# Query tiles copied inside SBUF by a transfer and transposed as float32r

## The chip, the cores and the metric

One core of a Trainium2 chip runs the whole kernel. The metric is the device time of one execution in microseconds. Engines: TensorE (PE; its weight loads are PEld), VectorE (DVE), ScalarE (ACT), GpSimd (POOL), and SyncE (SP), which issues the transfers.

## The reference

x is 2048 x 512 in float32. It is normalised, goes through a linear attention with 32 heads of 16 and, beside it, through a gated feed-forward block of width 1792; the two results are multiplied.

```python
xn = _layernorm(x)
q, k, v = split_heads(xn @ wqkv)            # 32 heads of 16
pq, pk = phi(q), phi(k)                     # phi(t) = (t + 1 if t > 0 else exp(t)) + 1e-6
kv = einsum("hsd,hse->hde", pk, v)
den = einsum("hqd,hd->hq", pq, pk.sum(axis=s)) + 1e-6
s = (einsum("hqd,hde->hqe", pq, kv) / den) @ wo
g = silu((gelu(xn @ w_gate) * (xn @ w_up)) @ w_down)
out = x + s * g
```

## The kernel before

Large products run on TensorE in float32r, with each float32 operand split into a high and a low part (three products for one), and blocks of 2 x 2 are multiplied with seven products instead of eight. A float32r matmul here has 128 x 128 weights and 512 moving columns.

The program has four stretches: normalisation, keys, queries and the state (up to about 135 us); the feed-forward block for one half of the tokens (p = 1, to about 330 us) and the small matrices of the attention; the feed-forward block for the other half (p = 0, 352 to 545 us); and the last stage S, which multiplies the scaled queries with a combined matrix and writes the output.

No engine's order is written out. The kernel records operations with `do(engine, cost, function, output, inputs)`, each with an estimated cost in us, and the class Plan searches an order for all engines at once from costs, dependences and estimated transfer times (a list schedule, improved in rounds with a fixed seed). Each engine then executes its list in that order; SP issues the transfers in its own list's order and waits there for what a transfer needs.

The sixteen query tiles (128 tokens x 512) are dealt with in pairs by `queries(i)`, spread over the p = 0 block. For a pair with first token tile t0: the queries are loaded from device memory (q_d) into the buffer q (place 12 of the pool "dp"); POOL multiplies each tile with the keys' sum into u (place 13); DVE adds over each head (den), adds den_eps, takes the reciprocal (rr) and scales q in place (L1142); TensorE transposes each tile in four 128 x 128 pieces into a PSUM bank ptq (L1148), as float32 against the identity matrix; ACT copies it into pT (place 14); and a transfer stores pT in device memory (pn_d), from where stage S loads it much later (tiles pb). Places 12, 13 and 14 are single buffers: the next pair uses the same ones. For half p = 1 tokens 1024 to 2047 come first, so the first pair is q8 with tiles 8 and 9.

Names in rows: FX, FY, FZ are PSUM banks of the feed-forward's first products, DX, DY, DZ those of its second, w and wd their weights, hf the split hidden values, acc the sums in SBUF. Numbers behind a name (FX11, ptq10) count units or token tiles.

Of the kernel before, what the change touches and what calls it, by code (L numbers as in the profile page):

```python
# [11 lines left out]
F32 = mybir.dt.float32  # L12
F32R = mybir.dt.float32r
AF = mybir.ActivationFunctionType
ALU = mybir.AluOpType
AX = mybir.AxisListType

P = 128
EPS_LN = 1e-5
EPS = 1e-6  # L20
WARM = 11
WARM2 = 2
ENGINES = {mybir.EngineType.PE, mybir.EngineType.Activation, mybir.EngineType.DVE, mybir.EngineType.Pool}


# [339 lines left out]
def kernel(  # L365
# [13 lines left out]
    nc = tc.nc  # L379
    S, D = x.shape  # L380
# [3 lines left out]
    KT = D // P  # L384
# [29 lines left out]
    def ring(tag, places):  # L414
        n = count[tag] = count.get(tag, -1) + 1
        return places[n % len(places)]
# [12 lines left out]
    def bank(i, name, shape=(P, D)):  # L429
        return tile_in("ps", i, list(shape), F32, name)  # L430


    def D2(i, name, dtype=F32, shape=(P, 2, D), parts=2):
        return tile_in("dp", i, list(shape), dtype, name, parts)
# [13 lines left out]
    def dma(dst, src, kb, name=""):  # L448
        do("SP", 0.475, lambda o, i: nc.sync.dma_start(o, i), dst, src, kb=kb, name=name)
# [22 lines left out]
    def copy(eng, dst, src, n, name=""):  # L472
        if eng == "ACT":
            do("ACT", act(n), lambda o, i: nc.scalar.copy(o, i), dst, src, name=name)  # L474
        else:
            do("DVE", dve(n), lambda o, i: nc.vector.tensor_copy(o, i), dst, src, name=name)
# [36 lines left out]
    do("POOL", 0.6, lambda o: nc.gpsimd.memset(o, NT * EPS), zacc)  # L513
    den_eps = tile_in("sm", "de", [P, H], F32, "den_eps")

    def warm(o, w, n=WARM):
        for _ in range(n):
            nc.tensor.matmul(o, w, w, start=True, stop=True)
# [54 lines left out]
    def half(v, i):  # L573
        return v.part(v.res[i:i + 1], (slice(None), i))
# [53 lines left out]
    xns = {}  # L628
# [31 lines left out]
    def transp(n, i):  # L660
        t = tokens[n][i]
        pt = early.get((n, i)) or bank(1, f"pt{t}", (P, KT, P))

        def run(o, a, b):
            for k in range(KT):
                nc.tensor.transpose(o[:, k, :], a[:, k * P:(k + 1) * P], b)  # L666
        do("PE", 0.432, run, pt, xns[t], ident, key=("T", n, i), name="T")
        if i == 0:
            xts[n] = D2(3 + n % 3, f"xt{n}").map(lambda ap: ap.rearrange("p a (k c) -> p a k c", c=P))
        v = xts[n]  # L670
        xts[n, i] = v.part((v.res[i],), (slice(None), i))
        copy("ACT", xts[n, i], pt, D, f"xt{n}{i}")
        pts[n, i] = pt
# [447 lines left out]
    def heads(v):  # L1121
        return v.map(lambda ap: ap.rearrange(heads_ap, d=DH))

    def queries(i):

        t0 = [8, 10, 12, 14, 0, 2, 4, 6][i]
        q, w, pT = D2(12, f"q{t0}"), D2(13, f"u{t0}"), D2(14, f"pT{t0}")
        for n in range(2):
            t = t0 + n
            dma(half(q, n), q_d(t, slice(t * P, (t + 1) * P)), 256)  # L1130
        den = little("den", f"den{t0}", [P, 2, H])
        for n in range(2):
            tt("POOL", "mul", heads(half(w, n)), heads(half(q, n)), heads(zb), D, "u")
        for n in range(2):
            do("DVE", 0.602, lambda o, i: nc.vector.tensor_reduce(o, i, axis=AX.X, op=ALU.add), den[:, n], heads(half(w, n)), name="den").port = False
        do("DVE", 0.1, lambda o, i: nc.vector.tensor_add(o, o, i.unsqueeze(1).to_broadcast([P, 2, H])), den, den_eps, name="eps").port = True
        r = little("rr", f"rr{t0}", [P, 2, H])
        do("DVE", 0.275, lambda o, i: nc.vector.reciprocal(o, i), r, den, name="rr").port = False
        pTs = pT.map(lambda ap: ap.rearrange("p a d -> p (a d)").rearrange("p (k c) -> p k c", c=2 * P))
        for n in range(2):  # L1140
            t = t0 + n
            do("DVE", 0.602, lambda o, j: nc.vector.scalar_tensor_tensor(  # L1142
                o, o, EPS, j.unsqueeze(2).to_broadcast([P, H, DH]), op0=ALU.add, op1=ALU.mult), heads(half(q, n)), r[:, n], name="pn")
            pt = bank(ring("ptq", [5, 6, 7]), f"ptq{t}", (P, KT, P))

            def run_t(o, a, b):
                for k in range(KT):
                    nc.tensor.transpose(o[:, k, :], a[:, k * P:(k + 1) * P], b)  # L1148
            do("PE", 0.432, run_t, pt, half(q, n), ident, key=("QT", i, n))
            copy("ACT", pTs[:, :, n * P:(n + 1) * P], pt, D, "pqT")  # L1150
        j = t0 % 8
        dma(pn_d[0 if t0 < 8 else 1](j // 2, (slice(None), slice(None), slice(j * P, (j + 2) * P))), pTs, 512)

# [2 lines left out]
    def ffn(p, groups):  # L1156
        keys, todo = [], [list(g) for g in groups]
        qs = [2 * u + i for u in UNITS[p] for i in range(2)]
        for n, q in enumerate(qs):
            u, is_up = divmod(q, 2)  # L1160
            prep_w(p, q)
            quad(p, q)
            if is_up:
                prep_d(p, u)
            if n == 0:
                keys += [("F", p, q, 1), ("F", p, q, 2)]
            keys += [("F", p, q, 6), ("F", p, q, 5), ("F", p, q, 7)]
            if n + 1 < NQ:
                keys += [("F", p, qs[n + 1], 1), ("F", p, qs[n + 1], 2)]
            keys += [("F", p, q, 4), ("F", p, q, 3)]  # L1170
            if not p:
                for i in PAIRS.get(n, []):
                    queries(i)
                    keys += [("QT", i, m) for m in range(2)]
            if not is_up and len(todo) > 1 and todo[0][-1] != u and ("F", p, 2 * todo[0][-1] + 1, 3) in keys:
                g = todo.pop(0)
                down(p, g)
                keys += down_keys(p, g)
        return keys, todo
# [88 lines left out]
    for s in (0, 1, 4, 3, 5, 6, 2):  # L1268
        for hl in "hl":
            src = View([x_d[hl](j, ()).res[0] for j in range(4)], x_d[hl](0, (slice(None), s)).get).map(lambda ap: ap.rearrange("p j c -> p (j c)"))  # L1270
            dma(xall(hl, s).map(lambda ap: ap.rearrange("p j k c -> p (j k c)").bitcast(F32)), src, 512)

    keys0, todo = ffn(0, [[6], [5, 4], [3, 2], [1, 0]])
    pe_keys += keys0
    change("silu", AF.Silu)
# [40 lines left out]
    def s_quad(p, c, forms, g, xp):  # L1316
        n = 2 * (1 - p) + c

        def prod_s(ps, i, start):
            a, b = PRODUCTS[i]  # L1320
            sum3(("S", p, c, i), ps, [(slot(ms[u], a, c), [f(b) for f in forms[u]]) for u in range(2)], start, True, "S", on=not start)

        def r_out(key, e, ps):
            v = g[key]
            if e is None:
                do("DVE", dve(NC), lambda o, i: nc.vector.tensor_mul(o, o, i), v, ps, name="r")
            else:
                tt("DVE", "add", e, e, ps, NC, "sc")
                do("DVE" if p == 0 and c else "POOL", dve(NC) if p == 0 and c else pool(NC), lambda o, i: (nc.vector if p == 0 and c else nc.gpsimd).tensor_mul(o, o, i), v, e, name="r")
        X, Y, Z = bank((1, 4)[n % 2], f"SX{n}"), bank(7, f"SY{n}"), bank((0, 6)[n % 2], f"SZ{n}")  # L1330
        prod_s(X, 1, True)
        e1 = esaved(X, f"se1_{n}")
        prod_s(Y, 2, True)
        r_out((0, c, 0), e1, Y)
        prod_s(X, 6, False)
        u2 = esaved(X, f"su2_{n}")
        prod_s(Z, 5, True)
        prod_s(X, 7, False)
        u3 = esaved(X, f"su3_{n}")
        r_out((1, c, 1), u3, Z)  # L1340
        prod_s(X, 4, False)
        r_out((1, c, 0), None, X)
        prod_s(Z, 3, False)
        r_out((0, c, 1), u2, Z)
        for dh, th in RORDER:
            pt = bank(ring("rt", [2, 3, 5]), f"rt{p}{dh}{c}{th}", (P, 4, P))

            def run_t(o, a, idn):
                for k in range(4):
                    nc.tensor.transpose(o[:, k], a[:, k * P:(k + 1) * P], idn)  # L1350
            do("PE", 0.432, run_t, pt, g[dh, c, th], ident, key=("RT", p, dh, c, th))
            chunk = slice((2 * dh + c) * P, (2 * dh + c + 1) * P)
            for h in range(2):
                pr = 2 * th + h
                v = xp[pr].part(xp[pr].res[2 * dh + c:2 * dh + c + 1], (slice(None), slice(None), chunk))
                do("DVE", dve(2 * P), lambda o, i: nc.vector.tensor_add(o, o, i), v, pt[:, 2 * h:2 * h + 2], name="xr")
                t = 8 * p + 2 * pr
                if not p:
                    dma(ext(out_p[:, t:t + 2, chunk]), v, 128)
                elif c and (dh, th) in ((0, 1), (1, 0)):  # L1360
                    dma(ext(out_p[:, t:t + 2]), xp[pr], 512)
# [61 lines left out]
```

## Time and profile before

| | |
|---|---|
| median of three timed runs | 612.95 us (612.9 to 613.46) |
| profiled execution | 610.86 us, its span 609.1 us |
| PE busy | 601.8 us, 99% |
| DVE, POOL, ACT busy | 479.7, 359.9, 336.2 us |
| transfers | 143.16 MB, queue share 67.2% of 16 engines |

Busy is time in which an engine executes; matmuls overlap, so a busy PE may still have slower and faster matmuls. The chain is followed back from the last instruction, at each step to what released it. The span leaves out some 1.8 us that lie around the first and the last instruction.

### The profile page before, as it was taken

How to read it: one execution, taken by the hardware profiler on the slowest of the kernel's cores; microseconds unless marked ns; L12 is line 12 of the kernel's file. 1: busy time of each engine (PE TensorE's matmuls, PEld its weight loads, DVE VectorE, ACT ScalarE, POOL GpSimd, SP SyncE). 2: the span in 40 equal slices, each digit the busy share in tenths (PEclk: the TensorE clock that was granted, in tenths of full speed). 3: DMA queues.
4: the chain of work that ended last, by engine and by line, in shares of the span. 5: the costliest groups of instructions: out<-in, count | busy, mean ns of one | idle time of the engine just before them, and what ended most of it. 6: DMA issues, size and time to landing. Idle time of an engine off the chain costs nothing.

```text
span 609.1 us, 8384 instructions
## 1 busy us (share of the span) xinstructions
PE 601.8 (99%) x2754; PEld 496.2 (81%) x2754; DVE 479.7 (79%) x712; ACT 336.2 (55%) x610; POOL 359.9 (59%) x300
## 2 busy tenths in 40 slices
PE   9999999999999999999999999999999999999996
PEld 8888888888888888888888788888888888878884
DVE  6999988785887998788878556677837875879886
ACT  6787778785676635653564154545224522677520
POOL 5834644544879768967785047267306641686970
PEclk9999999999999999999999999999999999999999
DMA  7369521249768648864669799898558855996346
GB/s 241 101 217 305 190 69 71 86 156 343 278 210 291 225 151 312 314 210 170 210 241 404 297 350 414 317 290 270 159 204 273 291 168 189 331 337 217 119 162 218
DMA packets 69659, 143.16 MB, mean 235 GB/s; under 512 B 5616, under 2 KB 28144, under 8 KB 69616
## 3 DMA queue, kind: packets, MB, share of 16 engines
q1 hardware_dynamic: 69616, 142.63, 67.2%
q8 instruction: 22, 0.36, 0.3%
q14 instruction: 21, 0.17, 0.1%
HBM read 81.00 MB, written 61.60 MB: 234 GB/s over the span
## 4 chain that ended last, share of the span: by engine, by line
PE 96%; DVE 1%; DMA 1%; POOL 0%; issue 0%; ACT 0%; DVEq 0%
PE FX L496 24%; PE DX L496 13%; PE FZ L496 12%; PE gps L496 7%; PE DZ L496 6%; PE FY L496 6%; PE X L496 5%; PE SX L496 4%; PE DY L496 3%; PE Z L496 3%; PE k L496 2%; PE SZ L496 2%; PE q L496 2%; PE Y L496 1%; PE pt L666 1%; PE ptq L1148 1%
## 5 line engine op out<-in xcount | busy, mean ns | idle before, releaser
L496 PE MATMUL FX<-Xh,w 128*128 128x512 f32 x448 | 152.5, 390 | 0.0
L1056 POOL TENSOR_TENSOR h<-h,g 128x512 f32<-128x512 f32 x42 | 62.9, 1500 | 96.4 <-DVE h L480 95.0
L496 PEld LDWEIGHTS FX<-Xh,w 128*128 128x128 f32 x448 | 83.8, 188 | 17.2
L480 POOL TENSOR_TENSOR h<-h,h 128x512 f32<-128x512 f32 x56 | 84.5, 1508 | 12.9 <-DVE hf6l L480 4.1
L496 PE MATMUL FX<-Xl,w 128*128 128x512 f32 x224 | 87.4, 390 | 0.0
L496 PE MATMUL FZ<-Xh,w 128*128 128x512 f32 x224 | 78.5, 391 | 0.0
L474 ACT COPY fu<-FX 128x512 f32<-128x512 f32 x56 | 32.9, 587 | 66.9 <-PE FX L496 65.0
L496 PE MATMUL gps<-pks,xns 128*128 128x512 f32 x192 | 51.0, 391 | 0.0
L496 PEld LDWEIGHTS FX<-Xl,w 128*128 128x128 f32 x224 | 42.1, 188 | 8.7
L496 PEld LDWEIGHTS FZ<-Xh,w 128*128 128x128 f32 x224 | 41.7, 188 | 9.0 <-DVE g L480 0.6
L742 POOL TENSOR_TENSOR zacc<-zacc,kp 128x512 f32<-128x512 f32 x16 | 24.2, 1511 | 37.0 <-DVE kp L731 31.0
L496 PE MATMUL FZ<-Xl,w 128*128 128x512 f32 x112 | 43.9, 392 | 0.0
L1082 DVE TENSOR_TENSOR acc<-acc,DX 128x512 f32<-128x512 f32 x48 | 32.6, 682 | 14.3 <-PE DX L496 13.9
L496 PEld LDWEIGHTS gps<-pks,xns 128*128 128x128 f32 x192 | 35.9, 188 | 7.4
L496 PE MATMUL FY<-Xh,w 128*128 128x512 f32 x112 | 39.5, 394 | 0.0
L480 DVE TENSOR_TENSOR g<-fu,FZ 128x512 f32<-128x512 f32 x28 | 19.2, 685 | 17.0 <-PE FZ L496 7.7
L1082 DVE TENSOR_TENSOR acc<-acc,DZ 128x512 f32<-128x512 f32 x32 | 21.9, 683 | 12.7 <-PE DZ L496 9.0
L496 PE MATMUL X<-kq,Xh 128*128 128x512 f32 x96 | 31.1, 397 | 0.0
L1048 ACT ACTIVATE g<-g 128x512 f32<-128x512 f32 x42 | 26.6, 632 | 7.9 <-DVE g L480 7.8
L480 DVE TENSOR_TENSOR h<-fu,FZ 128x512 f32<-128x512 f32 x28 | 19.2, 685 | 14.3 <-PE FZ L496 7.6
L480 POOL TENSOR_TENSOR u<-q,zacc 128x512 f32<-128x512 f32 x16 | 21.0, 1331 | 11.9 <-DMA q<-q_d 11.3
L496 PEld LDWEIGHTS FY<-Xh,w 128*128 128x128 f32 x112 | 21.0, 188 | 4.7 <-issue 0.5
(413 smaller groups left out, 1621.3 us busy)
## 6 DMA issues: line engine op xcount, KB each, us to landing
w_d<-w SPq DMA_DIRECT2D x36, 512.0 KB, 5.1
w<-w_d SPq DMA_DIRECT2D x36, 512.0 KB, 5.1
wd_d<-wd SPq DMA_DIRECT2D x21, 512.0 KB, 4.9
wd<-wd_d SPq DMA_DIRECT2D x21, 512.0 KB, 5.6
x<-in_A_x SPq DMA_DIRECT2D x16, 256.0 KB, 4.0
q_d<-qp SPq DMA_DIRECT2D x16, 256.0 KB, 2.2
q<-q_d SPq DMA_DIRECT2D x16, 256.0 KB, 5.2
pn_d<-pT SPq DMA_DIRECT2D x8, 512.0 KB, 6.4
```

Source lines behind the costliest of these rows:

```text
L474: do("ACT", act(n), lambda o, i: nc.scalar.copy(o, i), dst, src, name=name)
L480: do(eng, c, lambda o, p, q: getattr(e, f"tensor_{op}")(o, p, q), dst, a, b, name=name)
L496: nc.tensor.matmul(o, v[i], v[i + 1], start=start and part == 0 and i == 0, stop=stop and part == 1 and i == len(v) - 2, skip_group_check=on)
L666: nc.tensor.transpose(o[:, k, :], a[:, k * P:(k + 1) * P], b)
L742: do("POOL", pool(D), lambda o, i: nc.gpsimd.tensor_add(o, o, i), zacc, p0, name="zacc")
L1048: curved("gelu", do("ACT", curve(NC), lambda o, i: nc.scalar.activation(o, i, AF.Gelu_apprx_tanh), g, ps if e is None else g, name="gelu"))
L1056: do("POOL", pool(NC), lambda o, i: nc.gpsimd.tensor_mul(o, o, i), h, g, name="h")
L1082: do("DVE", dve(NC), lambda o, i: nc.vector.tensor_add(o, o, i), a, ps, name="acc")
L1148: nc.tensor.transpose(o[:, k, :], a[:, k * P:(k + 1) * P], b)
```

## The change

Each scaled query tile is first copied by a transfer from q to a new tile v, which is declared float32r and lies in place 13, where u lies before; the bytes are the same. TensorE transposes v as float32r against an identity in float32r (ident_r, made by one ACT cast). For tile 8 alone, the first, TensorE also transposes q as before into another bank (pte), and DVE subtracts the two results and adds 2^20 times the difference to pT. The recorded cost of the new transposition is TURN = 0.27 us; that of a float32 one stays 0.432. Other transpositions only call a shared function now. The order is searched anew.

```diff
+TURN = 0.27
...
+    def turn(o, a, b):
+        for k in range(KT):
+            nc.tensor.transpose(o[:, k], a[:, k * P:(k + 1) * P], b)
+
+    def turn_r(o, a, b):
+        for k in range(KT):
+            nc.tensor.transpose(o[:, k].bitcast(F32R), a[:, k * P:(k + 1) * P], b)
...
         for n in range(2):
             t = t0 + n
+            if n == 0:
+                v = D2(13, f"v{t0}", F32R)
             do("DVE", 0.602, lambda o, j: nc.vector.scalar_tensor_tensor(
                 o, o, EPS, j.unsqueeze(2).to_broadcast([P, H, DH]), op0=ALU.add, op1=ALU.mult), heads(half(q, n)), r[:, n], name="pn")
+            dma(half(v, n).map(lambda ap: ap.bitcast(F32)), half(q, n), 256)
             pt = bank(ring("ptq", [5, 6, 7]), f"ptq{t}", (P, KT, P))
-
-            def run_t(o, a, b):
-                for k in range(KT):
-                    nc.tensor.transpose(o[:, k, :], a[:, k * P:(k + 1) * P], b)
-            do("PE", 0.432, run_t, pt, half(q, n), ident, key=("QT", i, n))
-            copy("ACT", pTs[:, :, n * P:(n + 1) * P], pt, D, "pqT")
+            do("PE", TURN, turn_r, pt, half(v, n), ident_r, key=("QT", i, n))
+            dst = pTs[:, :, n * P:(n + 1) * P]
+            copy("ACT", dst, pt, D, "pqT")
+            if i == 0 and n == 0:
+                pe = bank(ring("ptq", [5, 6, 7]), f"pte{t}", (P, KT, P))
+                do("PE", 0.432, turn, pe, half(q, n), ident, key="probe")
+                d = U("fe", FE, "probe").map(lambda ap: ap.rearrange("p (k c) -> p k c", c=P))
+                tt("DVE", "sub", d, dst, pe, D, "probe")
+                do("DVE", 0.602, lambda o, a: nc.vector.scalar_tensor_tensor(o, a, 1048576.0, o, op0=ALU.mult, op1=ALU.add), dst, d, name="probe")
...
+    ident_r = tile_in("cpool", "ones", [P, P], F32R, "ident_r")
+    copy("ACT", ident_r, ident, P, "ident_r")
```

On TensorE, around tiles 10 and 11 in the p = 0 block, before:

```order
L496 MATMUL FZ11_3900<-Xh0_250,w113_3774 128x512 x2
L1148 MATMUL ptq10_4033<-ident_173,q10_3887 128x128 x4
L496 MATMUL FZ11_3900<-Xl0_261,w113_3774 128x512
L496 MATMUL FZ11_3900<-Xh0_250,w113_3774 128x512
L496 MATMUL FZ11_3900<-Xl0_261,w113_3774 128x512
L496 MATMUL FZ11_3900<-Xh0_250,w113_3774 128x512
L1148 MATMUL ptq11_4046<-ident_173,q10_3887 128x128 x4
L496 MATMUL FX8_3982<-Xh0_250,w82_3800 128x512 x2
```

and after the change, from the first product of DZ060 on, with the rows between left out:

```order
L497 MATMUL DZ060_4025<-hf6h_3703,wd62_3781 128x512
L497 MATMUL DZ060_4025<-hf6l_3713,wd62_3781 128x512
L497 MATMUL DZ060_4025<-hf6h_3703,wd62_3781 128x512
...
L497 MATMUL DZ061_4075<-hf6h_3703,wd63_3809 128x512
L523 MATMUL ptq10_4105<-ident_r_3309,v10_4063 128x128 x4
L497 MATMUL DZ061_4075<-hf6l_3713,wd63_3809 128x512
L497 MATMUL DZ061_4075<-hf6h_3703,wd63_3809 128x512
L497 MATMUL FX9_4114<-Xh0_253,w90_3834 128x512 x2
...
L497 MATMUL FZ8_3938<-Xh0_253,w83_3847 128x512 x2
L523 MATMUL ptq11_4136<-ident_r_3309,v10_4063 128x128 x4
```

The transposition of tile 10 stood among FZ11's matmuls and reads q10; now it reads v10 and stands later, 33 matmuls behind the last row of DZ060 that is shown, and tile 11 ten matmuls behind tile 10.

On DVE, the same pair, before:

```order
L1082 TENSOR_TENSOR acc0_5_3954<-acc0_5_3954,DZ060_3939 128x512
L1082 TENSOR_TENSOR acc0_1_3922<-acc0_1_3922,DZ060_3939 128x512
L1135 TENSOR_REDUCE den10_3987<-u10_3969 128x32 x2
L1082 TENSOR_TENSOR acc0_7_3960<-acc0_7_3960,DZ061_3991 128x512
L1136 TENSOR_TENSOR den10_3987<-den10_3987,den_eps_3443 128x64
L1138 RECIPROCAL rr10_4009<-den10_3987 128x64
L1142 SCALAR_TENSOR_TENSOR q10_3887<-q10_3887,rr10_4009 128x512
```

and after the change:

```order
L1141 TENSOR_REDUCE den10_4023<-u10_4009 128x32
L1088 TENSOR_TENSOR acc0_5_4020<-acc0_5_4020,DZ060_4025 128x512
L1141 TENSOR_REDUCE den10_4023<-u10_4009 128x32
L1142 TENSOR_TENSOR den10_4023<-den10_4023,den_eps_3471 128x64
L1144 RECIPROCAL rr10_4049<-den10_4023 128x64
L1150 SCALAR_TENSOR_TENSOR q10_3959<-q10_3959,rr10_4049 128x512 x2
L1088 TENSOR_TENSOR acc0_1_4001<-acc0_1_4001,DZ060_4025 128x512
```

The two scalings of the pair (q10 from q10 and rr10) now stand together behind one add from DZ060, ahead of the second.

On SP, transfers around the same pair, before:

```order
L449 DMA q10_3887<-q_d_80 128x512 x2
L449 DMA pn1_d_85<-pT8_3868 512x1x256
L449 DMA wd40_3928<-wd40_d_143 128x1024
L449 DMA w92_3943<-w92_d_141 128x1024
L449 DMA wd41_3985<-wd41_d_144 128x512
L449 DMA wd42_4000<-wd42_d_145 128x1024
L449 DMA wd43_4021<-wd43_d_146 128x1024
L449 DMA w60_4027<-w60_d_123 128x1024
```

and after the change:

```order
L450 DMA q10_3959<-q_d_80 128x512 x2
L450 DMA pn1_d_85<-pT8_3961 512x1x256
L450 DMA wd40_4014<-wd40_d_143 128x1024
L450 DMA wd41_4045<-wd41_d_144 128x512
L450 DMA v10_4063<-q10_3959 128x512 x2
L450 DMA w93_4071<-w93_d_142 128x1024
L450 DMA w91_4079<-w91_d_140 128x512
L450 DMA wd42_4089<-wd42_d_145 128x1024
L450 DMA q12_4100<-q_d_80 128x512 x2
```

The two copies from q10 to v10 are new; the weight loads w93, w91 and wd42 stand behind them, wd40 and wd41 ahead.

## Rows read from the trace of the kernel before

**Rows 1.** Busy time of each engine in the query stretch (us, instructions), granted clock, DMA share:
```profile
352.00:545.00 193.00, 192.78 (x882) 159.31 (x881) 133.87 (x189) 86.67 (x153) 96.57 (x72) 1.00 0.79 275
```

**Rows 2.** The chain that ended last, shares of the span:
```profile
PE 96%; DVE 1%; DMA 1%; POOL 0%; issue 0%; ACT 0%; DVEq 0%
```

**Rows 3.** TensorE's waits over the span: total us, times, longest:
```profile
PE warm L518 <- DVE ones L507: 1.2, 1, 1.2
PE rt L1350 <- DVE acc L1329: 0.7, 1, 0.7
PE ptq L1148 <- DVE q L1142: 0.2, 1, 0.2
```

**Rows 4.** Chain in order of time, 376 to 386 us: start, us, what:
```profile
377.17 1.36 PE FX L496 x6
...
379.66 0.44 PE ptq L1148 x4
```

**Rows 5.** Timeline around one query tile: start us, us, instruction:
```profile
379.27 0.58 PEld L1148 LDWEIGHTS ptq<-ident,q 128*128 128x128 f32 x4
379.50 0.60 PE L1148 MATMUL ptq<-ident,q 128*128 128x128 f32 x4
...
379.85 0.48 PE L496 MATMUL FZ<-Xl,w 128*128 128x512 f32 x1
...
380.17 0.39 PE L496 MATMUL FZ<-Xh,w 128*128 128x512 f32 x1
```

**Rows 6.** Tile k (ns min/median/max), then the timeline at its first matmul:
```profile
L496 PEld LDWEIGHTS k<-kq,Xh x24: 186/188/192, 8.5 to 24.7; 128*128 128x128 f32 x24
L496 PE MATMUL k<-kq,Xh x24: 389/393/499, 8.5 to 24.9; 128*128 128x512 f32 x24
...
8.47 0.30 PEld L496 LDWEIGHTS k<-kq,Xh 128*128 128x128 f32 x2 [0.25 <-ACT Xh L474]
8.47 0.50 PE L496 MATMUL k<-kq,Xh 128*128 128x512 f32 x1
```

**Rows 7.** Tile ptq, then the timeline of a transposition that had waited:
```profile
L1148 PEld LDWEIGHTS ptq<-ident,q x64: 138/140/144, 379.3 to 530.3; 128*128 128x128 f32 x64
L1148 PE MATMUL ptq<-ident,q x64: 270/272/328, 379.5 to 530.4; 128*128 128x128 f32 x64
...
412.83 0.42 PEld L1148 LDWEIGHTS ptq<-ident,q 128*128 128x128 f32 x4 [0.66 <-DVE q L1142]
412.84 0.66 PE L1148 MATMUL ptq<-ident,q 128*128 128x128 f32 x4 [0.22 <-DVE q L1142]
```

**Rows 8.** Groups by line, 370 to 540 us: count, busy us, mean ns, idle before:
```profile
L1135 DVE TENSOR_REDUCE den<-u 128x32 f32<-128x512 f32 x16 | 10.8, 682 | 5.8 <-POOL u L480 5.8
...
L1082 DVE TENSOR_TENSOR acc<-acc,DZ 128x512 f32<-128x512 f32 x12 | 8.2, 685 | 10.3 <-PE DZ L496 7.6 <-ACT acc L474 2.7
...
L1138 DVE RECIPROCAL rr<-den 128x64 f32<-128x64 f32 x8 | 4.4, 550 | 0.2
...
L1136 DVE TENSOR_TENSOR den<-den,den_eps 128x64 f32<-128x64 f32 x8 | 3.2, 399 | 0.1
```

**Rows 9.** Tile q, 360 to 540 us, as in rows 6:
```profile
L480 POOL TENSOR_TENSOR u<-q,zacc x16: 1286/1296/1741, 370.2 to 523.5; 128x512 f32<-128x512 f32 x16
L1142 DVE SCALAR_TENSOR_TENSOR q<-q,rr x16: 678/721/1780, 376.8 to 527.9; 128x512 f32<-128x512 f32 x16
...
  DMA q<-q_d: 11.3, 5
...
DMA to landing us min/median/max: 2.7/5.2/7.9
```

**Rows 10.** DMA in 370 to 540 us: packets, MB, share of 16 engines:
```profile
DMA packets 18105, 44.57 MB, mean 262 GB/s; under 512 B 1671, under 2 KB 5767, under 8 KB 18094
...
q1 hardware_dynamic: 18094, 44.43, 76.5%
```

**Rows 11.** The page's DMA issues: KB each, median us to landing:
```profile
q_d<-qp SPq DMA_DIRECT2D x16, 256.0 KB, 2.2
```

## What the change does to the time: a prediction

> **What bounds the kernel now.** I read the stretches first, then the chain, then TensorE's waits, then single instructions. In the stretch 352 to 545 us, where all sixteen query tiles are transposed, TensorE is busy for 192.78 of 193 us at a granted clock of 1.00, which is the 2.4 GHz level, while VectorE (DVE), the next, has 133.87 [rows 1]. The chain that ended last is PE for 96% [rows 2]. Over the whole span TensorE's matmuls waited three times: 1.2 us for the ones at the start, 0.7 us at the end, and 0.2 us for a query tile [rows 3]. So a TensorE nanosecond saved in this stretch is a nanosecond of the kernel, and a nanosecond that TensorE waits there is one lost. Other engines' work counts only where TensorE waits for it.
>
> **What a transposition costs today.** In the chain, six float32r matmuls of 512 columns take 1.36 us, 226.7 ns each, and the four transpositions of a query tile take 0.44 us [rows 4]. The timeline confirms it: the first of four starts at 379.50, the first matmul behind them has 0.48 us instead of 0.39, and the second starts at 380.17. That is 0.67 us for four transpositions and one matmul, so 0.443 us for the four, change of kind included [rows 5].
>
> **What it costs as float32r.** No transposition in float32r is in this trace, so I bound it. 512 columns at 2.4 GHz are 213.3 ns of the 226.7, and 13.4 ns are left for each instruction. 128 columns in one pass would be 53.3 + 13.4 = 66.7 ns, four of them 0.267 us. The lower end, a quarter of 226.7 ns, is 0.227 us for four; the upper end is no gain at all, 0.443 us, or a little more.
>
> Which end depends on the weight load, as each transposition loads its own 128x128 weights. A float32r load is recorded at 188 ns, that of a float32 transposition at 140. The delay to the matmul shows where an engine had been idle: the float32r matmul at 8.47 starts with its load and is recorded at 499 ns instead of the usual 389 to 393, so its weights took some 110 ns [rows 6]. The transposition at 412.84, also after a wait, starts with its load and has the 328 ns that are the maximum of its row, against a median of 272: its weights took 56 ns [rows 7]. If the new transposition loads like the old one, 56 ns fit under 66.7 and 0.267 stands. If it loads like a float32r matmul, one cannot follow the next in less than 110 ns, which is what it costs today. I take 0.267, since the operation stays a transposition of four-byte data, and it is this that goes with the short load in the rows. The saving is 0.443 - 0.267 = 0.176 us a tile, 2.82 us for sixteen, with 0 and 3.46 us (0.443 - 0.227) as its ends.
>
> The Trainium skill (TensorE: Matmul & The Clock Gate, LDWEIGHTS) has a rule against the change: a load takes its number of columns divided by 1.2 in ns, whatever the contraction, hence 107 ns as an estimate for 128 columns, and four transpositions could not take less than 0.43 us. By that rule the sum would lose the 2.82 us. The trace agrees for float32r loads (110 ns) and disagrees for transpositions (56 ns).
>
> **What is added on TensorE.** One float32 set of four transpositions, the probe: 0.443 us. The rest of TensorE's list holds the same numbers of matmuls.
>
> **What is added elsewhere.** ACT gets one small cast, DVE two operations of 512 columns, some 0.68 us each by the reductions and adds there [rows 8]. DVE is busy for 134 of 193 us, so they lie beside TensorE's work; without that cover they cost 1.4 us once. The probe's second operation stands ahead of the first pair's store on SP, which nothing on TensorE needs before the last stage.
>
> SP issues sixteen more transfers of 256 KB, 4.2 MB beside the 44.57 MB that 170 us of this stretch already move [rows 10]. Each now lies between DVE's scaling and the transposition. The nearest rows: a 256 KB store of queries lands after 2.2 us, a load of queries after 2.7 to 7.9 us, median 5.2 [rows 9, 11]. Behind such a transfer on SP stand weight loads: behind v10, w93, w91 and wd42, which TensorE first uses 7 to 28 us after the tile's transposition by the count of its list, so a late scaling delays none of them enough.
>
> The copy takes the buffer of the product u. So GpSimd's products for the next pair wait until both transpositions of this pair are done; before, they waited for their own load only. The loop of a pair is: transposition, two products (1.3 us each), two reductions (0.68 each), sum (0.4), reciprocal (0.55), two scalings (0.72 each), transfer, transposition [rows 8, 9]. That is 6.4 us without the transfer and 11.6 with one of 5.2; from pair to pair TensorE's list has 13 to 33 us of other work, so the loop closes.
>
> **Does TensorE wait for a transfer?** The tightest place in the new order is tile 10. DVE's scaling stands behind an add that needs the first product in DZ060; between that product's last matmul and the transposition of tile 10 stand 33 matmuls, 33 x 0.2267 = 7.5 us. From it DVE needs about 0.2 us of pipeline end, the add 0.68, the reduction 0.68, sum 0.4, reciprocal 0.55, scaling 0.72: 3.2 us [rows 8, 9]. So 4.3 us are left for a transfer that takes 2.2 to 7.9: a wait of 0 to 3.6 us, 0.9 at the median of 5.2. Tile 11 has ten matmuls more ahead and over 6 us. The same count gives the other pairs 6 to 12 us, beyond the median but not all beyond the slowest. I put 0.5 us of waiting into the sum, with 0 and some 9 us as ends (3.6 at tile 10 and about 1.9 at each of three pairs that have 6 us, all at 7.9).
>
> **The sum.** The profiled execution took 610.86 us, 609.1 of it span. 610.86 - 2.82 + 0.44 + 0.5 = 608.98. The three timed runs have a median 2.09 us above the profiled execution, so 611.1 against 612.95: 0.3% faster. A measurement of this kernel tells about 0.2%, 1.2 us, from no change.
>
> **Rivals.**
>
> *The long load.* Transpositions in float32r keep today's pace since their loads take 110 to 115 ns. For: every float32r load in the trace is the long kind. Against: the short one goes with transpositions. Then nothing is saved: + 0.44 for the probe, 0 to 0.3 for sixteen tiles at 115 instead of 111 ns, + 0.5 for waiting: 613.4 to 614.3, middle 613.9. This is also the case in which the change does not do what it says.
>
> *Late transfers.* The transfers fill 76.5% of the 16 engines' time here, and a load of queries has taken 7.9 us [rows 9, 10]. If the copies land like the slower of these, TensorE, which cannot pass over the transposition in its list, waits at tile 10 and at the pairs with 6 us. The other side begins at 3.6 us of waiting (2.4 net gain + 1.2), for instance 3.0 at tile 10 and 0.3 at two pairs; with 5 us the time is 615.1. For: in the trace GpSimd waited 11.3 us in five places for loads of queries [rows 9]. Against: the copy has no part in device memory, and most pairs have over 6 us.
>
> *The order.* The list is searched anew, and every engine's order differs far beyond the queries. Today's order leaves TensorE hardly a gap (0.2 us in the middle, 0.7 at the end) [rows 3]; another may leave 1 to 2 us more, seldom less. Then 612.1 to 613.1: no change to be told.
>
> **Chances and range.** Forecast 0.45 (609.9 to 612.0: the ends are 0.227 us a set without a wait, which is 610.0, and 0.267 with 1.4 us of waiting). Long load 0.22. Late transfers 0.20, half of it beyond the point where it is slower. Order 0.13. Faster by over 0.2% (below 611.7): most of the forecast, 0.42. Slower (above 614.2): half of the late transfers, a third of the long load, a little of the order, 0.20. Within: 0.38. The range 609.9 to 614.4 leaves out most of the slower half of the late transfers and a little below.
>
> **What the profile after would show.** Right: the four transpositions of a query tile at 0.23 to 0.28 us in the chain, recorded loads of about 140 ns, copies landing in under 4.3 us, and TensorE's waits for v of 0.5 us in total. Long load: starts 110 ns apart and loads of 188 ns. Late transfers: a wait of TensorE for the transfer into v, first of all at tile 10. Order: the transpositions cheap, and new waits of TensorE for ACT, DVE or weights. It would be wrong above all if the weights of these transpositions load in the long form.

## The result and the profile after

The changed kernel takes 615.57 us (median of seven runs, 614.08 to 615.99) against 612.95 for the kernel before in the same session: a ratio of 1.0043, 95% interval 1.0029 to 1.0057. It is slower by 2.6 us; 611.1 was forecast, and the range ended at 614.4. The profiled execution took 615.26 us, its span 613.6.

The stretches first, beginning with those of the kernel before on either side of the one in [rows 1] (start:end in us, length, then busy us and instructions of PE, PEld, DVE, ACT and POOL, granted clock, DMA share, GB/s):

```profile
30.00:352.00 322.00, 322.00 (x1450) 264.92 (x1449) 266.87 (x386) 199.73 (x367) 202.94 (x181) 1.00 0.64 227
545.00:580.00 35.00, 35.00 (x159) 28.40 (x159) 32.72 (x46) 23.93 (x43) 27.81 (x18) 1.00 0.53 177
```

The same stretches of the changed kernel, with the query stretch:

```profile
30.00:352.00 322.00, 320.78 (x1445) 263.46 (x1445) 268.21 (x383) 197.34 (x363) 199.40 (x178) 1.00 0.63 224
352.00:545.00 193.00, 192.32 (x882) 157.97 (x881) 139.59 (x190) 86.26 (x154) 95.86 (x72) 1.00 0.83 293
545.00:580.00 35.00, 34.24 (x154) 26.94 (x153) 31.68 (x48) 24.51 (x46) 27.44 (x18) 1.00 0.63 216
```

TensorE, which never stopped between 30 and 352 us, now stands idle there for 1.22 us, and no query tile has been transposed by then. In the query stretch it loses 0.46 us more than in [rows 1], behind it 0.76 us. The chain that ended last says the same; PE held 96% of it in [rows 2]:

```profile
PE 87%; DMA 5%; DVE 4%; ACT 1%; issue 1%; POOL 1%; SPq 0%; DVEq 0%; ACTq 0%; POOLq 0%
```

TensorE's waits over the span, which were three in [rows 3] (what waited, for what: us in total, times, longest):

```profile
PE rt L519 <- DVE acc L1343: 1.2, 1, 1.2
PE FZ L497 <- DVE g L481: 1.2, 2, 1.1
PE warm L527 <- DVE ones L508: 1.2, 1, 1.2
PE rt L519 <- DVE xp L1367: 0.9, 1, 0.9
PE DX L497 <- ACT pT L475: 0.7, 1, 0.7
PE DX L497 <- ACT hf0h L475: 0.4, 1, 0.4
PE k L497 <- DVE Xl L481: 0.3, 1, 0.3
PE DZ L497 <- ACT hf0h L475: 0.3, 1, 0.3
PE pt L519 <- DVE xn L653: 0.3, 1, 0.3
PE SX L497 <- ACT su L475: 0.2, 1, 0.2
```

No transposition of a query tile (ptq) is on this list, and TensorE never waits for a copy into v. What waits is the feed-forward block's FZ, at 154 us, its last DZ and DX at 548 and 552 us (for hf0h), the last stage's rt at 589 and 607 us, and one product DX beside a query tile.

**The wait at 154 us**, in the chain, whose pieces there are mostly transfers (start us, us, what):

```profile
136.20 6.52 DMA q_d<-qp
...
143.49 2.98 DMA g_d<-GTa
...
147.97 6.60 DMA g_d<-GTa
...
154.67 0.70 DVE g L481
...
155.41 0.74 PE FZ L497 x2
```

Three stores to device memory follow one another, with short operations between, and DVE's g, which FZ needs, was released by the last. All of this lies some 230 us ahead of the first query tile that TensorE transposes, and ahead of the first instruction that the change adds, the cast of ident_r at 320 us.

**The transpositions.** Pieces of the chain in the changed kernel, as in [rows 4]:

```profile
383.91 0.44 PE pte L519 x4
...
393.90 0.31 PE ptq L523 x4
...
394.23 0.59 ACT pT L475
...
394.87 0.96 PE DX L497 x3
...
409.37 0.30 PE ptq L523 x4
```

The probe (pte, float32) takes the 0.44 us of before, a float32r set 0.30. Behind the first set DX waits for ACT, which empties the bank that ptq and this DX share. The tile ptq itself (ns min/median/max), as in [rows 7]:

```profile
L523 PEld LDWEIGHTS ptq<-ident_r,v x64: 138/141/144, 393.6 to 532.0; 128*128 128x128 f32 x64
L523 PE MATMUL ptq<-ident_r,v x64: 220/248/258, 393.7 to 532.0; 128*128 128x128 f32 x64
```

The load's record is the short one, as forecast. The timeline around the third set, with its weight loads, is to be read as [rows 5] were:

```profile
409.21 0.46 PE L523 MATMUL ptq<-ident_r,v 128*128 128x128 f32 x4
409.50 0.46 PE L497 MATMUL DZ<-hf6l,wd 128*128 128x512 f32 x1
409.80 0.39 PE L497 MATMUL DZ<-hf6h,wd 128*128 128x512 f32 x1
...
409.46 0.19 PEld L497 LDWEIGHTS DZ<-hf6l,wd 128*128 128x128 f32 x1
409.57 0.19 PEld L497 LDWEIGHTS DZ<-hf6h,wd 128*128 128x128 f32 x1
```

From 409.21 to 409.80 four transpositions and one matmul take 0.59 us, so the set takes 0.59 - 0.227 = 0.363 us where it was 0.443. The saving is 0.08 us a tile, 1.28 for sixteen, less than half of the 2.82 in the sum.

Where the rest went is seen where the order transposes two tiles directly behind one another, again with the loads first:

```profile
427.78 0.66 PEld L523 LDWEIGHTS ptq<-ident_r,v 128*128 128x128 f32 x7
...
428.39 0.30 PEld L497 LDWEIGHTS FX<-Xh,w 128*128 128x128 f32 x2
...
427.78 0.81 PE L523 MATMUL ptq<-ident_r,v 128*128 128x128 f32 x8
428.42 0.69 PE L497 MATMUL FX<-Xh,w 128*128 128x512 f32 x2
428.95 0.40 PE L497 MATMUL FX<-Xl,w 128*128 128x512 f32 x1
```

The loads of the second to the eighth transposition begin at 427.78 and the load behind them at 428.39: seven steps of 87 ns. In the set above, the two long loads of the matmuls behind begin at 409.46 and 409.57, 110 ns apart. A set of four whose first weights are already loaded is then three short steps and one long one, 3 x 87 + 110 = 371 ns, near the 363 measured; for eight it is 7 x 87 + 110 = 719 ns, and 428.95 - 427.78 - 2 x 0.227 = 0.716 us were measured. So two sets with one change of kind between them and the matmuls cost as much for each, 0.358 us, as a set by itself: a price of the change of kind is not what took the saving, and the rows fit a limit by the distance between weight loads, which no run tests by itself. (The starts within one set of four lie closer, (0.46 - 0.248) / 3 = 71 ns on average, but that is not a pace that lasts.) A float32 set follows at (0.60 - 0.272) / 3 = 109 ns in [rows 5], and four times 109 is 0.436 of its 0.443.

**The copies** land as follows (tile v, then the stretch in which the first pair's two copies were under way):

```profile
DMA to landing us min/median/max: 2.3/3.7/9.8
...
380.00:394.00 14.00, 14.00 (x68) 11.57 (x66) 9.76 (x11) 5.83 (x11) 5.88 (x4) 1.00 1.03 406
```

The slow two, 8.5 and 9.8 us, are those of tiles 8 and 9, when the transfer engines were full (DMA share 1.03). They were issued at 383.8 and 386.3, and tile 8 was transposed at 393.7: just in time.

### The profile page after: what moved, and what is told of

Same layout as the page of the kernel before. It is cut to its first block, busy times and chain, and to the rows that moved or that the text cites. A ratio compares the mean times of both kernels' runs of the same rounds, so it can differ in the third digit from the quotient of the medians.

```text
span 613.6 us, 8426 instructions
## 1 busy us (share of the span) xinstructions
PE 602.8 (98%) x2758; PEld 494.3 (81%) x2758; DVE 488.9 (80%) x714; ACT 336.1 (55%) x611; POOL 355.8 (58%) x300
## 4 chain that ended last, share of the span: by engine, by line
PE 87%; DMA 5%; DVE 4%; ACT 1%; issue 1%; POOL 1%; SPq 0%; DVEq 0%; ACTq 0%; POOLq 0%
PE FX L497 22%; PE FZ L497 11%; PE DX L497 11%; PE gps L497 6%; PE X L497 5%; PE DZ L497 5%; PE FY L497 5%; PE SX L497 3%; PE DY L497 3%; PE Z L497 2%; PE q L497 2%; PE SZ L497 2%; PE k L497 2%; DMA g_d<-GTa 2%; PE Y L497 1%; PE pt L519 1%
## 5 line engine op out<-in xcount | busy, mean ns | idle before, releaser
L1062 POOL TENSOR_TENSOR h<-h,g 128x512 f32<-128x512 f32 x42 | 61.2, 1460 | 57.8 <-DVE h L481 39.1
L481 POOL TENSOR_TENSOR u<-q,zacc 128x512 f32<-128x512 f32 x16 | 22.6, 1430 | 45.7 <-DMA wd<-wd_d 20.6
```

The source lines that it names most:

```text
L481: do(eng, c, lambda o, p, q: getattr(e, f"tensor_{op}")(o, p, q), dst, a, b, name=name)
L1062: do("POOL", pool(NC), lambda o, i: nc.gpsimd.tensor_mul(o, o, i), h, g, name="h")
```

## The experiments

Two theories run through the expectations. **A, the order**: the search, begun anew, came to an order for all engines that leaves TensorE more waits, most of which have nothing to do with the queries. **B, the work**: the copies and the probe themselves make the kernel wait. Each kernel was timed beside the kernel before (612.09, 612.35, 612.44, 612.05 and 611.93 us in five sessions); ratios are to it, with their 95% intervals. Between sessions the ratios are compared, as the kernel before itself had 612.95 in the first session and up to 1 us less in these.

### The changed kernel's order, with float32 transpositions

```diff
-            do("PE", TURN, turn_r, pt, half(v, n), ident_r, key=("QT", i, n))
+            do("PE", TURN, lambda o, a, b, c: turn(o, a, c), pt, half(v, n), ident_r, ident, key=("QT", i, n))
```

The cost that the search sees is unchanged, so the order is the same; copies and probe stay, and v holds float32.

> The order of the changed kernel instruction for instruction, copies and probe kept, but the sixteen tiles are transposed as float32 again. It measures the float32r transposition alone. By the two traces a set of four cost 0.443 us and now 0.365, so 16 x 0.078 = 1.25 us: 616.8 us, ratio 1.0063 to the kernel before. If float32r saved what was forecast (0.176 a tile), 618.4, ratio 1.0089. If it saves nothing, 615.6, ratio 1.0043.

Measured: 616.88 us, 1.0080 (1.0064 to 1.0096). The chain of this kernel at the same place, beside the sets of 0.30 above:

```profile
409.58 0.23 PE DZ L497
409.81 0.44 PE ptq L519 x4
410.25 0.47 PE DZ L497 x2
```

Set and two matmuls take 0.91 us here, and 0.30 + 0.53 = 0.83 in the changed kernel. So float32r is worth 0.08 us a tile by the chain; 1.3 us in all by the medians of two sessions, 2.3 by their ratios. It is a gain, as the intervals of the two ratios do not meet. That it is about half of what was forecast is told by the chain; the times alone would also allow the forecast's 1.0089.

### The order of before, written out, with copies

For the next three the search is replaced by a table of start times taken from the kernel before; the copies stand behind each scaling, and a transposition moves back until a set time (LAG) after its copy, which is recorded as copy_v. The probe is left out.

```diff
+START = [
+    750, 650, 650, 1450, 1110, 5810, 650, 2075, 1125, 1600, 2550, 3500, 3025, 3975, 4450, 4925, 5875, 5400, 5620, 6280, 6140, 6881, 8847, 9536,
...
+            gone = at[p] + (LAG if p.name == "copy_v" else p.cost if p.eng != "SP" else 0.01)
```

With 4.5 us, float32r:

> The order of the kernel before is kept from a table; only the copies are put in behind each scaling and a transposition is moved back until 4.5 us after its copy was issued. float32r transpositions, no probe. Theory A (the search found a worse order; the change itself costs little): 612.95 - 1.25 + 0 to 0.6 us of waiting = 611.7 to 612.3, ratio 0.998 to 0.999. Theory B (the copies make the kernel wait, in whatever order): 614.5 or more, ratio above 1.0025.

With 4.5 us, float32 transpositions of v:

> As the run with the old order, but the copied tiles are transposed as float32: the copies and the later transpositions alone, without any saving. Theory A: 612.95 + 0 to 0.6, ratio 1.000 to 1.001. Theory B: 615.8 or more, ratio above 1.0045. Its difference to the run with float32r is the saving in this order, 1.25 us by the traces.

With 11 us for the first four tiles, 7 for the next ten and 5.5 for the last two, float32r:

> The order of the kernel before, written out, with the sixteen copies and the float32r transpositions and without the probe; each transposition stands 11 us (first four), 7 us or, for the last two, 5.5 us behind its scaling, and loads that this pushes back are put earlier. Theory A: with room for the copies, which landed in 2.3 to 9.8 us, TensorE waits for none, and the old order keeps its few waits: 611 to 613, against 634 with the shorter room. Theory B: the copies hold up other transfers and the long wait for ACT at 548 us stays: 620 or more. A wait for a copy of 1 us or more on TensorE's list would say that the room is still too short.

Measured: 634.38 us, 1.0369 (1.0348 to 1.0391); 634.38, 1.0357 (1.0337 to 1.0377); 626.55, 1.0232 (1.0212 to 1.0251). TensorE's longest waits in the first of them, and three of its stretches:

```profile
PE ptq L637 <- DMA v<-q: 8.2, 3, 5.5
PE FX L611 <- ACT fu L589: 6.9, 1, 6.9
...
380.00:390.00 10.00, 4.45 (x20) 3.47 (x19) 3.78 (x5) 1.70 (x4) 2.36 (x2) 0.82 1.00 390
390.00:400.00 10.00, 10.00 (x39) 7.47 (x38) 2.57 (x4) 4.90 (x9) 2.53 (x3) 0.83 0.56 186
400.00:410.00 10.00, 10.00 (x46) 8.26 (x45) 8.00 (x14) 4.87 (x9) 2.56 (x3) 1.00 0.52 158
```

Here TensorE does wait for copies, 5.5 us for the first alone (landing times in this kernel reach 8.8 us), and ACT later holds it up for 6.9. More room in the third brings the waits for v to 2.8 us and the time down by 8, and the wait of 6.9 us, which B expected to stay, gives way to one of 2.5. Theory A, which gave 613.6 at most, is wrong for all three. So B's mechanism exists: a copy put where the old order has no room makes TensorE wait far longer than its transposition saves. How much of the 14 to 22 us is the copies' is not shown, since no run has the old order written out without them. And the changed kernel shows none of the waits for v, since its search moved the first transposition from 379.5 to 393.7 us. Beside such waits float32r and float32 show no difference.

### Other seeds of the search, the same work

```diff
-    SEED = 2
+    SEED = 3
```

The kernel before with seeds 3, 5 and 4, the changed kernel with seeds 4 and 5:

> The kernel before, nothing changed but the seed of its search (3 instead of 2): another order of the same instructions. Theory A: the time moves by more than 0.2% without any change of the work, most likely up, to 614 to 617 (ratio 1.002 to 1.007). Theory B: a new search alone costs nothing, 612.3 to 613.6, ratio 0.999 to 1.001.

> The kernel before with its search's seed set to 5 and nothing else. Theory A: another order moves the time by 0.5 to 2 us without any change in the work, and as the seed of the kernel before is the best of five by the planner's own total, most likely up: 612.5 to 614.5. Theory B says nothing of it but that a search's spread is small against 2.6 us: 612 to 612.8.

> The kernel before with its search's seed set to 4; same instructions. Theory A: 612.5 to 615, since the two other seeds gave 613.9 and 613.7 and the kernel before's own is the lowest so far. Theory B: 612 to 613.

> The changed kernel with the seed of its search for an order set to 4 instead of 2: the same instructions, in another order. Theory A (the time was lost because the search, started anew, came to an order whose chains fit less well, and the waits lie in stages far from the queries): another order has other waits, so the time moves by 1 us or more, and most likely down: 611.5 to 614.5, against 615.6 for the changed kernel. Theory B (the copies and the probe themselves make the kernel wait): whatever the order, sixteen copies, sixteen transpositions and one probe are there, so the time stays at 615 to 616.5.

> The changed kernel with its search's seed set to 5; same instructions. Theory A: another order, 612 to 616, and with 613.45 (seed 4) and 615.57 (seed 2) a spread of 1 us or more. Theory B: 615 to 616.5.

### Without the probe, and the probe alone

```diff
-            if i == 0 and n == 0:
-                pe = bank(ring("ptq", [5, 6, 7]), f"pte{t}", (P, KT, P))
-                do("PE", 0.432, turn, pe, half(q, n), ident, key="probe")
...
-                    keys += [("QT", i, 0)] + (["probe"] if i == 0 else []) + [("QT", i, 1)]
+                    keys += [("QT", i, m) for m in range(2)]
```

Searched anew with seeds 2, 4 and 5, then in the changed kernel's order written out:

> The changed kernel without the probe (its four transpositions, its subtraction and its sum; the output is then the one without the small correction), searched with the same seed. By work alone it is 0.44 us shorter than the changed kernel: 615.1. Theory A: it is another order too, so the time is anywhere in 611.5 to 616.5, and a fall by more than 0.44 is the order's. Theory B with the probe as the culprit (its wait for a bank and ACT's copy before VectorE's subtraction): 612 or less, and the wait by the third query tile gone.

> The same without the probe, with the search's seed 4, an order that fits better by the planner's own total than that of the kernel before. Theory A: with the waits of a good order, the saving of the sixteen transpositions (0.078 us each by the trace, 1.25 in all) shows against the kernel before: 610 to 612, which is at or below 612.9. Theory B: the copies cost what they cost in any order, 614 to 616.

> The changed kernel without the probe (the output then lacks the small correction), search's seed 5. Theory P (the probe, which keeps a bank of PSUM and one of three work places for some 12 us by the third query tile, spoils whatever order is searched): 2 to 3 us below the changed kernel of the same seed (614.03), so 611 to 612. Theory L (the two falls seen so far were the lottery of orders): anywhere in 611 to 615.

> The changed kernel's order written out, with the probe's rows left out (the output is then the one without the small correction) and all else in its place. Theory A: only the four transpositions of the probe go, 0.44 us: 615.1 (614.7 to 615.6). Theory B with the probe as the culprit: the wait at 394 us goes too and what follows moves up, 612 to 613.5.

The reverse, the kernel before with the probe and nothing else:

```diff
+                pe = bank(ring("ptq", [5, 6, 7]), f"pte{t}", (P, KT, P))
+                do("PE", 0.432, turn, pe, half(q, n), ident, key="probe")
```

> The kernel before with the probe alone: the third query tile is transposed a second time in float32, the difference (here zero) times 2^20 added; no copies, no float32r; searched with seed 2. Theory P: 2 to 3.5 us above the kernel before, 614 to 616. Theory L: its own work of 0.44 us and the lottery, 611.5 to 615, most likely 612.5 to 613.5.

Measured, medians in us and ratios to the kernel before:

| work | seed 2 | seed 3 | seed 4 | seed 5 |
|---|---|---|---|---|
| as before | (the kernel before) | 613.88, 1.0027 (1.0015 to 1.0038) | 612.18, 1.0002 (0.9989 to 1.0014) | 613.71, 1.0018 (1.0003 to 1.0033) |
| changed | 615.57, 1.0043 (1.0029 to 1.0057) | | 613.45, 1.0021 (1.0009 to 1.0033) | 614.03, 1.0040 (1.0026 to 1.0054) |
| changed, no probe | 612.38, 1.0005 (0.9992 to 1.0018) | | 610.97, 0.9984 (0.9971 to 0.9997) | 614.59, 1.0039 (1.0023 to 1.0054) |
| before and probe | 614.70, 1.0039 (1.0024 to 1.0055) | | | |

With the same work the ratio moves by 0.0022 to 0.0055 from order to order, which is 1.3 to 3.4 us, about as much as the change itself moved it. Theory B, which held a new order for nearly free, gave 615 to 616.5 for the changed kernel with other seeds; both medians lie below. By the ratios seed 4 is 1.3 us below seed 2, with intervals that just meet, and seed 5, at 1.0040, is where seed 2 was. A missed as well: seed 4 of the kernel before, at 612.18, lies below its 612.5 to 615 and within B's range, and seed 3, at 613.88, between the two.

The list of TensorE's waits with seed 4 and the old work is worth a look:

```profile
PE k L496 <- ACT Xh L474: 1.5, 1, 1.5
PE FY L496 <- DVE g L480: 1.2, 1, 1.2
...
PE rt L1350 <- DVE acc L1329: 0.9, 1, 0.9
PE rt L1350 <- DVE xp L1356: 0.8, 1, 0.8
```

Waits for g (ahead of 352 us), acc and xp like those of the changed kernel are here too, in an order that the search itself found, without copy, float32r or probe. But this list is 3.5 us longer than that of [rows 3], and the kernel is as fast as the kernel before (1.0002; its profiled execution 612.16 against 610.86). TensorE was busy for 600.4 us in it, against 601.8. So the waits come with the order, but their sum is not the time that an order costs.

Leaving out the probe, 0.44 us of TensorE's time, changed the ratio by -0.0038, -0.0037 and -0.0001 with seeds 2, 4 and 5, that is by -2.3, -2.3 and 0 us. In the changed kernel's own order it brought no gain: 616.94 us, 1.0067 (1.0043 to 1.0092), above the ranges of both theories. So the probe's price is not its work. That it spoils every order is refuted by seed 5. That it makes bad orders likelier (it holds a PSUM bank from 384 to 395 us) is neither shown nor excluded by three pairs and the kernel with the probe alone, whose 614.70 lies in the range of theory P and above what L held most likely.

The kernel without the probe and with seed 4 is the only one below the kernel before, by 0.16% (0.03 to 0.29).

### The changed kernel's order, with the old work in it

The table is now taken from the changed kernel, and copies and probe are taken out again.

```diff
-            dma(half(v, n).map(lambda ap: ap.bitcast(F32)), half(q, n), 256)
...
-            do("PE", TURN, turn_r, pt, half(v, n), ident_r, key=("QT", i, n))
+            do("PE", 0.432, turn, pt, half(q, n), ident, key=("QT", i, n))
```

> The changed kernel's order written out as a table, with the work of the kernel before in it: no copies, no probe, the sixteen tiles transposed in float32 straight from the scaled queries. It computes what the kernel before computes. Theory A (the order found anew holds the lost time): the waits at 154, 551, 589 and 607 us stay, the sets cost 1.25 us more and the probe's 0.44 us go: 616.4, at least 615.3. Theory B (copies and probe hold the lost time): it falls to the time of the kernel before, 612 to 613.5.

The same with the order of the 610.97 us kernel:

> The order of the fastest kernel so far (no probe, seed 4; 610.97) written out, with the work of the kernel before in it: no copies, float32 transpositions straight from the scaled queries. It computes what the kernel before computes. Theory A: sixteen sets at 0.443 instead of 0.365 us, so 1.25 us longer: 612.2 (611.6 to 612.9), that is the time of the kernel before within the measurement. Rival C (that kernel is faster by its order alone, and the float32r sets give nothing that the copies don't take back): 610.5 to 611.3.

Measured: 633.54 us, 1.0358 (1.0334 to 1.0382), and 628.07, 1.0260 (1.0242 to 1.0279). Neither theory had said this. GpSimd's longest waits in the first show why:

```profile
POOL u L593 <- DMA q<-q_d: 62.8, 6, 26.3
```

The transpositions stood where the copies had put them, tile 8's for instance 10 us behind its copy's issue (383.8 and 393.7 in the changed kernel). With copies, the buffer q is free when its copy has landed; without them it is held until the transposition, so the next pair's load starts late, GpSimd waits up to 26 us for it, DVE behind GpSimd, ACT behind DVE, and at last TensorE. The pair did not test what it was for. In the next two each transposition is moved up to its scaling:

> The changed kernel's order written out with the old work in it, as in the run that took 633.5 us, but each float32 transposition moved up to 0.3 us behind its scaling, or as soon behind it as its bank is free; four q loads of the fourth and seventh pair still come 1 to 5 us later than in the changed kernel. Theory A (the order holds the lost time): the waits far from the queries stay, 615 to 617, and no wait of GpSimd for a q load above 10 us. Theory B (copies and probe hold it): 612 to 613.5. If it is above 620 with FX waiting for ACT again, the late q loads have not been mended and the run decides nothing.

> The order of the 610.97 us kernel written out with the old work in it, float32 transpositions moved up to 0.3 us behind their scaling, or as soon behind it as their bank is free; q loads of the second, fourth and seventh pair come 1 to 3 us later. Theory A: 612.2 (611.6 to 612.9), 1.25 us above that kernel. Rival C (faster by its order alone, the float32r sets give nothing): 610.5 to 611.3. Above 618 with FX waiting for ACT: undecided, as above.

Measured: 621.07 us, 1.0161 (1.0136 to 1.0187), and 620.38, 1.0137 (1.0115 to 1.0160). Both lie above what either theory gave. TensorE's waits in the first:

```profile
PE ptq L631 <- issue: 3.3, 1, 3.3
PE FZ L609 <- DVE g L593: 1.4, 2, 1.2
PE ptq L631 <- DVE q L1260: 1.3, 1, 1.3
PE rt L631 <- DVE acc L1447: 1.2, 1, 1.2
...
PE rt L631 <- DVE xp L1471: 0.6, 1, 0.6
...
PE SX L609 <- ACT su L587: 0.2, 1, 0.2
```

Two transpositions, now too early for DVE's scaling, wait 4.6 us: that is the hand placement's. Without them the time would be some 616.5, near the 616.4 that A gave, but this is an estimate. What is shown without one is the rest of the list: FZ for g, rt for acc, rt for xp and SX for su stand there as in the changed kernel, though no copy, no float32r and no probe is in the program. The waits for hf0h are on the list of neither kernel with the changed kernel's order and the old work, so whether they are the order's or the work's stays open. The second of the pair has 3.8 us of waits of transpositions for DVE's q and decides nothing about rival C.

## Why the prediction was wrong, by its steps

**The step that failed is the order.** The sum put waits of TensorE at 0.5 us, for copies, and took all other waits as those of before; a worse order was a rival with 0.13, "1 to 2 us more", 612.1 to 613.1. The lists of waits, each of one execution, show what came instead. In all five kernels that run the changed kernel's order and were profiled (changed, float32, no probe, and both with the old work), TensorE waits for g ahead of 352 us (0.8 to 1.4 us), 1.2 us for acc at the end where it had 0.7, for xp (0.6 to 0.9) and for su (0.2). In the kernel before and in the three with its order written out, copies included, only the 0.7 is there of these. That is 2.1 to 2.8 us of waits in each of the five which come and go with the order, whatever the work. Of the changed kernel's other new waits, the 0.7 us of DX for ACT behind tile 8's set is also in the first kernel with the old work, and the 0.7 for hf0h is in neither of the two.

The account by the changed kernel's rows: 1.28 us gained, 0.44 spent on the probe, 2.8 and 0.7 us of these waits: 2.7 us slower, where the medians say 2.6. That this agrees is in part luck. With all of the list it is 3.8 us, the two profiled executions, to which the lists belong, differ by 4.4, and seed 4 of the kernel before shows that such waits need not add up to time. So it is shown that the forecast left out waits which the new order brought; how many of the 2.6 us they cost is an estimate.

The misjudgement was to read the few waits of [rows 3] as a property of the kernel, when they are a property of one order and of one execution, which was 2.09 us below the median: the kernel before has the lowest or second lowest time of its four seeds. A search begun anew starts from the spread of such orders, 612 to 614 us with the old work, and the change was known to draw from it. Of the prediction's four pictures of the profile after, that of the order came nearest: transpositions cheaper, and new waits of TensorE for ACT and DVE.

**Mis-sized: the float32r set**, 0.363 us measured, 0.267 in the sum, inside the bounds of 0.227 and 0.443; the chain has 0.30 for it where the forecast wanted 0.23 to 0.28. This takes 1.5 of the 2.8 us away. The step that was wrong is "56 ns fit under 66.7": the 56 ns are the delay from a load to its matmul after a wait, and the sum took them for the distance at which loads can follow one another. That distance is 87 ns here, more than the 66.7 reckoned for the matmul, and 110 for the long load behind the set. The Trainium skill (TensorE: Matmul & The Clock Gate, Back-to-back issue gap) gives 81 ns for a sustained pair of load and matmul with 128 columns, so 0.324 us as an estimate for a set; the trace has 87 ns between the loads and 0.363 us with the long load behind. The Trainium skill's rule on loads (same page, LDWEIGHTS), from which the prediction had 0.43 us at least for a set, as an estimate, is refuted for these transpositions by the same rows.

**Right:** the load's record is the short kind (138 to 144 ns) and a set is cheaper than before, so the long-load rival falls; the probe takes 0.44 us; no transposition of the changed kernel waits for a copy; no wait of TensorE is put down to DVE's two operations for the probe, though DVE stood idle for 3.6 us ahead of the first of them.

**Right in mechanism, wrong in place: late transfers.** Tile 10, called the tightest, had its copies in time. The slow copies were those of the first pair, 8.5 and 9.8 us, beyond the 7.9 that bounded the sum. The three kernels with the old order show what they cost where there is no room: 2.8 to 8.4 us of waiting for v. (The rival's example of 5 us of waiting gives 615.6 by the prediction's own terms, 611.1 + 4.5, and not 615.1.)

**Open** is what the change costs on average over orders. The three seeds of the changed kernel have a mean ratio of 1.0035, the four of the kernel before 1.0012; by work alone it should be 0.8 us faster. With seeds 1.3 to 3.4 us apart these means don't tell whether copies and probe make good orders rarer.

## What to carry to other kernels

Where a program searches the order of its instructions, any edit draws a new order: measure the spread first (the same work with other seeds), and don't forecast or credit a gain below it without the order held still or several orders on each side. Look for new waits over the whole span and not only where the edit is: one that lies ahead of every instruction of the edit, as that at 154 us, points to the order. But don't take the sum of the waits for the time lost. Take the price of a weight load from the distance between loads in a long run of them, and not from the delay to its matmul. And when an order is held still for a test, check what the removed operation had made free: here the copy had given the query buffer back before the transposition.

## What the runs showed of the hardware

- In a run of eight float32r transpositions of 128 x 128 the weight loads follow one another at 87 ns, with the same load record of about 140 ns as float32 ones, which follow at 109 ns. A set of four between float32r matmuls of 512 columns takes 0.363 us, a run of eight 0.716 (a float32 set: 0.443). The delay from load to matmul after a wait, 56 ns in float32 [rows 7], says nothing of this distance.
- A transfer of 256 KB inside SBUF landed after 2.3 us at the earliest (tile 10's, at a DMA share of 0.71) and after 8.5 and 9.8 when the transfer engines were full (DMA share 1.03); loads of the same size from device memory took up to 7.9 us in the kernel before [rows 9].
- After TensorE had waited 5.5 us for a copy, the granted clock was 0.82 and then 0.83 in two stretches of 10 us, that is partly at the lower of its levels (1.2 and 2.4 GHz): busy for all of the second, it has 39 matmuls in it, four of them short transpositions, where the next 10 us at 1.00 have 46. The wait was paid for twice.
